# An attention and gate kernel on one core: the values of the first batch earlier in the order, and new weights of the order

## The chip, the cores and the metric

One core of a Trainium2 chip runs one program. Its engines are TensorE (PE, matmuls), VectorE (DVE), ScalarE (ACT), GpSimd (POOL) and SyncE (SP, which here issues all DMAs). Each engine works through its own list of instructions in order and waits on semaphores for the others. The metric is the device time of one execution in microseconds; the median of three runs before the change is 1022.07 us (1021.38 to 1022.09).

## The reference, cut to what matters

```python
kv_pool = kv.reshape(B, H//4, 4, W//4, 4, C).mean(axis=(2, 4))
kv_flat = kv_pool.reshape(B, -1, C) @ w_sr      # 768 keys, k = v
s = (q @ k.transpose(0, 2, 1)) / sqrt(C)
a = softmax(s)                                  # 1e-9 added to the sum
x = a @ v
gate = sigmoid(causal convolution of x with 5 taps per channel)
out = (gate * (x @ w_val)) @ w_out
```

There are 4 batches of 12288 queries and 128 channels, all in float32. Each batch has its own 768 keys, which are its values too.

## The kernel before, in words

The queries of a batch are cut into 24 groups of 512, and a group into 4 tiles of 128. For a tile PE makes the scores against 768 keys in six matmuls (L534): the high half of the query by the high and by the low half of the keys, and the low half of the query by the high half of the keys. The scores stay in one of three PSUM buffers (`s`). DVE takes their negative maximum (`nm`, L546), ACT the exponential and its sum (L553), DVE two small steps to the reciprocal (`r`, L562 and L567). ACT then writes the scaled high half in 16 bits (`hl`, L581), and DVE the low half (L592), after which the PSUM buffer is free. When two tiles are done, a DMA transpose (L605) on SP turns both halves into `pt`. When a group's two transposes have landed, 18 AV matmuls (L677) multiply by the high and the low half of the values (`vh`, `vl`). ACT copies the result to `x` (L695). GpSimd makes the five taps and adds them (`tap`, `gate`, L738 and L746; it also makes the low half of the query, `ql`, L520), ACT takes a tanh (`th`, L761), PE the value projection (`val`, L765), DVE their product (`h`, L769), PE the output projection (L774), and ACT the copy to `o` (L779), which SP stores. In the last groups DVE or PE make the taps and PE some of the transposes.

Per batch there is a `setup`. SP loads 16 pieces of `kv`; DVE (L307), and for some pieces of the first batch GpSimd (L326), sums each 4x4 window; PE projects (L360); ACT and DVE write the halves of the keys (`kh` L376, `kl` L400), and ACT the projected values as they are (`vt`, L388). The chain from there to the halves of the values is: `big`, the largest magnitude of each channel (DVE, L431); three steps on one column (L434, L436 and L438) that make a power of two `pw` and its inverse `up`; `diag`, the identity scaled by `up` (ACT, L423), and `wb`, the weights scaled by `pw` (ACT, L427); then for each half of the keys six matmuls of `vt` by `diag` (PE, L453), the high half `vh` (ACT, L463) and the low half `vl` (DVE, L474). The second half takes the same PSUM bank as the first.

The order of each engine's list is written by a planner (`Plan.order`) while the program is built. Every step has an engine, an estimated duration, a due time, the steps it comes after and the buffers it takes and frees. The planner goes forward in its own time. On each engine, among the steps that could begin within `WAIT` of the earliest one, it takes the one with the lowest due time. On SP a copy that follows a copy has `CLUMP` taken off its due time, so copies stay together. The due time of a step of a group is the group's number times `PERIOD`, plus its entry in `DUE` (four entries, one per tile, for the softmax steps, with a quarter of a period more for each). Loads and stores are placed on a grid of `PERIOD` and may not start before it. In `setup` the chain of the first batch has the due time `vals0` and an earliest start, `FIRST_VALS`:

```python
late = D["vals0"] if first else due(D["vals"])
s = plan.add("DVE", 0.87, late, lambda: v.tensor_reduce(
    out=big, in_=st["vt"], axis=AX.X, op=ALU.max, apply_absolute_value=True), vts,
    start=FIRST_VALS if first else 0.0)
...
by["wb"] = plan.add("ACT", 0.25, late + (20.0 if first else 1.0), wb, [s, weights_done], takes=("wb",))
```

Of the kernel before, what the change touches and what calls it, by code (L numbers as in the profile page):

```python
# [19 lines left out]
PIECES = 16  # L20
PARTS = 2

PERIOD = 9.97
DUE = dict(keys=-39.58, vals=-35.42, vals0=17.37, q=-44.21, qh=4.86, ql=-80.97,
           score=(-7.47, -6.32, -5.63, -6.47), max=(-23.77, -6.1, 13.1, -11.57),
           exp=(0.09, -30.82, -8.74, -13.77), hi=(-29.44, -20.58, 0.7, -43.56),
           lo=(22.34, -32.12, 5.51, 24.31), turn=(-11.32, 15.47, 2.1, 15.6), pe=6.0, thi=29.07,
           tlo=-11.13, r=(-50.81, -28.34, -47.73, -28.55), grid=-1.12, av=20.41, avs=4.86,
           halo=63.51, x=42.45, gate=30.41, th=53.25, val=47.33, h=-3.27, out=11.86, evac=21.59,
           store=52.32, end_diag=-56.57, end_gate=26.44, end_th=54.36, end_val=54.8, end_h=-26.7,  # L30
           end_out=56.32, end_evac=-38.92)

# [12 lines left out]
class Plan:  # L47
# [2 lines left out]

    EDGE = 0.04
    LAG = dict(PE=0.16, ACT=0.1, DVE=0.085, POOL=0.04, SP=0.0)
    WAIT = dict(PE=0.07, ACT=0.26, DVE=0.12, POOL=0.07, SP=0.8)
    DMA_LEAD, DMA_TAIL, CLUMP = 1.3, 0.8, 16.23

    def __init__(self):
        self.steps, self.stock = [], {}
# [14 lines left out]
    def order(self):  # L72
# [12 lines left out]
        while any(ready.values()):  # L85
            best = None
            for e, items in ready.items():
# [8 lines left out]
                if not ests:  # L96
                    continue
                t0 = min(t for t, _ in ests)
                s = min((s.due - (s.kind == last[e] == "copy") * self.CLUMP, n, s)
                        for n, (t, s) in enumerate(ests) if t <= t0 + self.WAIT[e])[2]  # L100
                t0 = next(t for t, x in ests if x is s)
# [52 lines left out]
def attn_moe_kernel(ctx, tc, qT, kvT, w_sr, w_moe, outT):  # L154
# [12 lines left out]
    HALO = TAPS - 1  # L167
    T = PERIOD
    D = DUE
    scale = 1.0 / float(C) ** 0.5  # L170
# [690 lines left out]

ON_PE, IN_S = 2, 4
TAIL, LAST, LAST_TURNED = 4, (2, 1, 1), ((), (0,), (0,))
FIRST_VALS, KEYS_BY = 26.0, -5
FIRST_Q = {0: 17.0, 1: 17.5, 2: 18.0, 4: 26.0}
SPARE, FOLDED = (6, 7, 8), (3, 5, 8, 10, 12)
TURNED = ((),)
# [28 lines left out]
```

## Time and profile before

| what | value |
|---|---|
| median of 3 runs | 1022.07 us |
| profiled execution | 1022.09 us, span 1020.2 us |
| busy, share of the span | PE 97%, DVE 91%, POOL 91%, ACT 87% |
| chain that ended last | PE 78%, POOL 5%, DVE 2%, ACT 1% |
| granted clock, mean | 0.995 |

The span is the time from the first to the last instruction; the rest of the profiled execution lies around it. A share of busy time is a mean over the whole span. The chain that ended last is followed back from the last instruction, at each step to what released it.

### The profile page before, as it was taken

How to read it: one execution, taken by the hardware profiler on the slowest of the kernel's cores; microseconds unless marked ns; L12 is line 12 of the kernel's file. 1: busy time of each engine (PE TensorE's matmuls, PEld its weight loads, DVE VectorE, ACT ScalarE, POOL GpSimd, SP SyncE). 2: the span in 40 equal slices, each digit the busy share in tenths (PEclk: the TensorE clock that was granted, in tenths of full speed). 3: DMA queues.
4: the chain of work that ended last, by engine and by line, in shares of the span. 5: the costliest groups of instructions: out<-in, count | busy, mean ns of one | idle time of the engine just before them, and what ended most of it. 6: DMA issues, size and time to landing. Idle time of an engine off the chain costs nothing.

```text
span 1020.2 us, 15459 instructions
## 1 busy us (share of the span) xinstructions
PE 991.6 (97%) x4586; PEld 606.9 (59%) x4586; DVE 930.5 (91%) x1806; ACT 884.9 (87%) x1584; POOL 930.6 (91%) x1069
## 2 busy tenths in 40 slices
PE   4799999999999999999999999999999999999998
PEld 3555555556555666656665656555666566666655
DVE  6899999999999999999999999999989898898984
ACT  1788889989898998999899989998999989999884
POOL 5179999999999999999999999999999999999994
PEclk9799999999999999999999999999999999999999
DMA  8699999999999999999999999999999999999983
GB/s 321 122 241 234 229 230 269 232 238 244 212 251 244 223 232 253 245 218 238 224 241 226 233 248 230 232 248 231 186 216 217 201 207 224 206 211 190 186 176 93
DMA packets 616994, 227.05 MB, mean 223 GB/s; under 512 B 595536, under 2 KB 596304, under 8 KB 616912
## 3 DMA queue, kind: packets, MB, share of 16 engines
q1 hardware_dynamic: 616912, 226.07, 103.2%
q8 instruction: 37, 0.61, 0.3%
q14 instruction: 45, 0.37, 0.1%
HBM read 50.66 MB, written 25.17 MB: 74 GB/s over the span
## 4 chain that ended last, share of the span: by engine, by line
PE 78%; POOL 5%; DVE 2%; ACT 1%; issue 0%; POOLq 0%; ACTq 0%; DVEq 0%
PE s L534 33%; PE av L677 30%; PE m L774 7%; PE m L765 7%; POOL gate L746 2%; POOL tap L738 1%; DVE hl L592 1%; POOL ql L520 1%; ACT hl L581 0%; DVE nm L546 0%; POOL gate L738 0%; PE m L453 0%; PE m L360 0%; ACT s L553 0%; PE s L824 0%
## 5 line engine op out<-in xcount | busy, mean ns | idle before, releaser
L746 POOL TENSOR_TENSOR gate<-gate,tap 128x512 f32<-128x512 f32 x376 | 481.7, 1281 | 10.0
L592 DVE SCALAR_TENSOR_TENSOR hl<-s,r,hl 128x768 f16<-128x768 f32 x382 | 386.2, 1012 | 30.9 <-ACT hl L581 29.8
L553 ACT ACTIVATE s<-s,nm 128x768 f32<-128x768 f32 x384 | 336.3, 876 | 49.7 <-DVE nm L546 49.1
L546 DVE TENSOR_REDUCE nm<-s 128x1 f32<-128x768 f32 x384 | 362.8, 946 | 17.3 <-PE s L534 16.2
L677 PE MATMUL av<-pt,vh 128*128 128x512 f16 (+2 forms) x1176 | 370.8, 377 | 0.5 <-ACT s L553 0.5
L581 ACT ACTIVATE hl<-s,r 128x768 f16<-128x768 f32 x382 | 339.6, 907 | 26.7 <-DVE r L567 15.8
L534 PE MATMUL s<-kh,qh 128*128 128x512 f32 (+1 forms) x768 | 261.0, 421 | 11.0 <-DVE hl L592 8.1
L738 POOL TENSOR_SCALAR tap<-x,wb 128x512 f32<-128x512 f32 x376 | 254.6, 698 | 0.0
L677 PE MATMUL av<-pt,vl 128*128 128x512 f16 (+2 forms) x588 | 220.1, 375 | 0.0
L534 PEld LDWEIGHTS s<-kh,qh 128*128 128x128 f32 x768 | 132.2, 191 | 130.2 <-issue 54.9
L534 PE MATMUL s<-kl,qh 128*128 128x512 f32 (+1 forms) x768 | 199.5, 341 | 0.0
L534 PE MATMUL s<-kh,ql 128*128 128x512 f32 (+1 forms) x768 | 198.3, 339 | 0.0
L677 PEld LDWEIGHTS <-vh 128*128 128x128 f16 x1176 | 107.5, 98 | 142.6 <-issue 55.4
L520 POOL TENSOR_TENSOR ql<-q,qh 128x512 fp32r<-128x512 f32 (+1 forms) x98 | 122.8, 1254 | 28.1 <-ACT qh L516 28.1
L534 PEld LDWEIGHTS s<-kh,ql 128*128 128x128 f32 x768 | 119.2, 190 | 17.4
L534 PEld LDWEIGHTS s<-kl,qh 128*128 128x128 f32 x768 | 119.1, 190 | 17.5 <-DVE kl L400 0.2
L774 PE MATMUL m<-h,wm 128*128 128x512 f32 x188 | 99.0, 608 | 0.2 <-DVE h L769 0.2
L677 PEld LDWEIGHTS <-vl 128*128 128x128 f16 x588 | 57.7, 98 | 68.3 <-issue 22.1
L765 PE MATMUL m<-x,wb 128*128 128x512 f32 x188 | 96.0, 592 | 0.0
L738 POOL TENSOR_SCALAR gate<-x,wb 128x512 f32<-128x512 f32 x94 | 65.5, 697 | 28.0 <-ACT x L695 27.7
L567 DVE RECIPROCAL r<-r 128x1 f32<-128x1 f32 x384 | 62.9, 164 | 13.1
L779 ACT ACTIVATE o<-m 128x512 f32<-128x512 f32 x94 | 56.2, 598 | 17.7 <-PE m L774 16.8
(67 smaller groups left out, 617.8 us busy)
## 6 DMA issues: line engine op xcount, KB each, us to landing
q<-in_q SPq DMA_DIRECT2D x47, 512.0 KB, 5.4
out<-o SPq DMA_DIRECT2D x47, 512.0 KB, 3.3
kvt<-in_kv SPq DMA_DIRECT2D x60, 384.0 KB, 4.2
pt<-hl SPq DMA_TRANSPOSE x191, 5.9
o<-in_kv SPq DMA_DIRECT2D x3, 384.0 KB, 8.3
q<-in_q SPq DMA_DIRECT2D x2, 256.0 KB, 5.8
kvt<-in_kv SPq DMA_DIRECT2D x2, 192.0 KB, 4.4
raw<-in_w_moe SPq DMA_DIRECT2D x1, 261.0 KB, 2.9
```

Of the source, the lines that this page charges most:

```text
L520: nc.gpsimd.tensor_tensor(out=g.ql, in0=g.io.q[:, mine], in1=g.qh.bitcast(F32), op=ALU.subtract)
L534: nc.tensor.matmul(t[:, c0:c1], a[:, sl], k[:, c0:c1], start=(i == 0), stop=(i == 2))
L546: v.tensor_reduce(out=s.tile, in_=sc.tile[:, :NK], axis=AX.X, op=ALU.max, negate=True)
L553: nc.scalar.activation(out=sc.tile[:, :NK], in_=sc.tile[:, :NK], func=AF.Exp, bias=mx.tile, accum_out=sc.tile[:, NK:NK + 1])
L567: v.reciprocal(out=s.tile, in_=e.tile)
L581: nc.scalar.activation(out=g.hls[j // 2][:, half, 0], in_=sc.tile[:, :NK], func=AF.Copy, scale=r.tile)
L592: v.scalar_tensor_tensor(out=hl[:, half, 1], in0=sc.tile[:, :NK], scalar=r.tile, in1=hl[:, half, 0], op0=ALU.mult, op1=ALU.subtract)
L677: nc.tensor.matmul(g.av, st[name][:, k * P:(k + 1) * P], g.pt[:, :, a * NCH + k], start=(i == 0), stop=(i == len(AV) - 1))
L738: nc.gpsimd.tensor_scalar(out=s.tile, in0=src(k), scalar1=wt(k), scalar2=1.0, op0=ALU.mult, op1=ALU.mult)
L746: nc.gpsimd.tensor_tensor(out=g.gate, in0=g.gate, in1=tap.tile, op=ALU.add)
L765: nc.tensor.matmul(g.m, st["wb"][:, :C], g.x[:, HALO:], start=True, stop=True)
L774: nc.tensor.matmul(g.m2, wout, g.h, start=True, stop=True)
```

## The change

Nothing that is computed changes, and no instruction is added or taken away. The due times, the period, two of the planner's constants and the earliest start of the first batch's chain from `vt` to `vh` and `vl` have other values. `vals0` goes from 17.37 to -59.66 and `FIRST_VALS` from 26 to 22.

```diff
-PERIOD = 9.97
-DUE = dict(keys=-39.58, vals=-35.42, vals0=17.37, q=-44.21, qh=4.86, ql=-80.97,
-           score=(-7.47, -6.32, -5.63, -6.47), max=(-23.77, -6.1, 13.1, -11.57),
-           exp=(0.09, -30.82, -8.74, -13.77), hi=(-29.44, -20.58, 0.7, -43.56),
-           lo=(22.34, -32.12, 5.51, 24.31), turn=(-11.32, 15.47, 2.1, 15.6), pe=6.0, thi=29.07,
-           tlo=-11.13, r=(-50.81, -28.34, -47.73, -28.55), grid=-1.12, av=20.41, avs=4.86,
-           halo=63.51, x=42.45, gate=30.41, th=53.25, val=47.33, h=-3.27, out=11.86, evac=21.59,
-           store=52.32, end_diag=-56.57, end_gate=26.44, end_th=54.36, end_val=54.8, end_h=-26.7,
-           end_out=56.32, end_evac=-38.92)
+PERIOD = 9.88
+DUE = dict(keys=-39.84, vals=-44.67, vals0=-59.66, q=-43.31, qh=-7.04, ql=-78.0,
+           score=(-7.1, -5.53, -6.34, -6.81), max=(-25.34, -9.07, 9.14, -15.56),
+           exp=(-3.41, -25.85, -12.4, -10.65), hi=(-37.79, -19.35, -1.17, -39.39),
+           lo=(21.28, -36.39, 7.1, 23.79), turn=(-9.59, 6.75, 10.86, 17.01), pe=3.81, thi=36.11,
+           tlo=-12.72, r=(-51.78, -33.05, -44.37, -42.65), grid=-0.11, av=19.88, avs=6.14,
+           halo=69.09, x=41.55, gate=30.73, th=60.74, val=47.67, h=-6.87, out=21.42, evac=28.89,
+           store=50.37, end_diag=-61.96, end_gate=34.22, end_th=46.53, end_val=51.12,
+           end_h=-30.5, end_out=51.42, end_evac=-42.17)
...
-    WAIT = dict(PE=0.07, ACT=0.26, DVE=0.12, POOL=0.07, SP=0.8)
-    DMA_LEAD, DMA_TAIL, CLUMP = 1.3, 0.8, 16.23
+    WAIT = dict(PE=0.06, ACT=0.29, DVE=0.12, POOL=0.05, SP=0.77)
+    DMA_LEAD, DMA_TAIL, CLUMP = 1.3, 0.8, 3.87
...
-FIRST_VALS, KEYS_BY = 26.0, -5
+FIRST_VALS, KEYS_BY = 22.0, -5
```

## Rows read from the trace of the kernel before

**Rows 1.** The page, busy time of PE, of its weight loads, and of DVE, ACT and POOL: us, share of the span, instructions.

```profile
PE 991.6 (97%) x4586; PEld 606.9 (59%) x4586; DVE 930.5 (91%) x1806; ACT 884.9 (87%) x1584; POOL 930.6 (91%) x1069
```

**Rows 2.** Busy time by stretch. Columns: stretch, its length, then for PE, PEld, DVE, ACT and POOL the busy us and, in brackets, the instructions; PE's granted clock (1.00 is 2.4 GHz), the DMA share, GB/s.

```profile
25.00:60.00 35.00, 26.83 (x113) 19.58 (x112) 29.80 (x58) 25.26 (x46) 7.50 (x8) 0.85 0.76 164
60.00:100.00 40.00, 38.03 (x177) 22.71 (x177) 37.33 (x76) 34.90 (x62) 37.58 (x43) 1.00 1.04 224
100.00:140.00 40.00, 39.13 (x178) 22.78 (x176) 38.54 (x76) 35.22 (x64) 38.62 (x44) 1.00 1.10 237
140.00:980.00 840.00, 839.43 (x3879) 509.61 (x3879) 784.58 (x1518) 760.79 (x1360) 808.63 (x916) 1.00 1.07 226
980.00:1020.00 40.00, 37.12 (x205) 22.91 (x204) 24.82 (x46) 23.96 (x47) 25.08 (x32) 1.00 0.52 128
```

**Rows 3.** What PE waited for: us in total, times, longest. The first line is of the stretch from 22 to 60 us, the others of that from 60 to 160 us.

```profile
PE s L534 <- DVE hl L592: 6.6, 4, 3.2
...
PE s L534 <- DVE hl L592: 1.5, 3, 0.9
PE s L534 <- DVE r L562: 1.1, 1, 1.1
```

**Rows 4.** What DVE waited for from 25 to 60 us, in the same columns.

```profile
DVE nm L546 <- PE s L534: 4.9, 5, 1.3
```

**Rows 5.** Single instructions on PE in order of time: start, us, engine, line, operation, out<-in, form, count, and in brackets the idle time ahead of it and what ended that.

```profile
31.67 0.98 PE L534 MATMUL s<-kh,qh 128*128 128x512 f32 x2 [3.24 <-DVE hl L592]
...
43.85 1.03 PE L453 MATMUL m<-diag,vt 128*128 128x128 f32 x6
...
48.17 0.61 PE L534 MATMUL s<-kh,qh 128*128 128x512 f32 x2 [1.19 <-DVE r L562]
...
49.83 0.62 PE L534 MATMUL s<-kh,qh 128*128 128x512 f32 x2 [0.35 <-DVE hl L592]
...
50.98 0.39 PE L677 MATMUL av<-pt,vh 128*128 128x512 f16 x1
...
52.17 0.59 PE L534 MATMUL s<-kh,qh 128*128 128x512 f32 x2 [0.15 <-DVE r L562]
...
771.38 0.38 PE L677 MATMUL av<-pt,vh 128*128 128x512 f16 x1
```

**Rows 6.** Busy time by stretch as in rows 2; the third column from the end is PE's granted clock.

```profile
22.00:28.00 6.00, 6.00 (x22) 4.87 (x23) 2.74 (x5) 3.26 (x7) 3.79 (x3) 1.00 0.27 102
28.00:34.00 6.00, 2.76 (x10) 2.17 (x9) 4.70 (x13) 4.27 (x7) 0.00 (x0) 0.72 0.32 96
...
46.00:52.00 6.00, 4.42 (x22) 2.87 (x22) 5.55 (x11) 5.34 (x11) 1.27 (x1) 1.00 0.90 204
```

**Rows 7.** Single instructions on DVE in order of time, columns as in rows 5.

```profile
25.54 0.96 DVE L546 TENSOR_REDUCE nm<-s 128x1 f32<-128x768 f32 x1 [1.32 <-PE s L534]
...
29.67 0.93 DVE L431 TENSOR_REDUCE big<-vt 128x1 f32<-128x768 f32 x1
30.52 1.93 DVE L592 SCALAR_TENSOR_TENSOR hl<-s,r,hl 128x768 f16<-128x768 f32 x2
...
33.97 0.96 DVE L546 TENSOR_REDUCE nm<-s 128x1 f32<-128x768 f32 x1 [1.20 <-PE s L534]
...
39.12 0.13 DVE L438 TENSOR_SCALAR up<-pw 128x1 int32<-128x1 int32 x1
...
50.55 0.55 DVE L474 TENSOR_TENSOR vl<-m,vh 128x384 f16<-128x384 f32 x1
```

**Rows 8.** Single instructions on ACT in order of time, columns as in rows 5.

```profile
29.26 1.70 ACT L581 ACTIVATE hl<-s,r 128x768 f16<-128x768 f32 x2
...
40.93 0.41 ACT L423 ACTIVATE diag<-ident,up 128x128 f32<-128x128 f32 x1
...
44.92 0.48 ACT L463 CAST vh<-m 128x384 f16<-128x384 f32 x1 [0.82 <-PE m L453]
...
57.60 0.60 ACT L695 ACTIVATE x<-av 128x512 f32<-128x512 f32 x1 [0.51 <-PE av L677]
```

**Rows 9.** Issues of DMA transposes on SP in order of time: start of the issue, us, engine, line. The first is the second of group 0, the other the second of group 71.

```profile
40.21 3.65 SPq L605 DMA_TRANSPOSE pt<-hl  x1
...
758.70 3.61 SPq L605 DMA_TRANSPOSE pt<-hl  x1
```

**Rows 10.** DMA issues by form: out<-in, engine, operation, count, median us from issue to landing.

```profile
pt<-hl SPq DMA_TRANSPOSE x191, 5.9
```

**Rows 11.** The chain that ended last, in order of time, in the fourth batch: start, us, engine, tile, line, matmuls.

```profile
961.07 0.43 PE av L677 x2
...
962.56 1.31 PE av L677 x6
...
964.98 2.17 PE av L677 x10
...
971.05 0.43 PE av L677 x2
```

**Rows 12.** The same chain in the tail.

```profile
1002.01 0.81 ACT pt L650
...
1003.79 0.94 DVE gate L720
...
1005.38 1.12 PE m L774 x2
```

## The prediction

> **What bounds the kernel now.** I read the busy shares first, then stretches of the span, then who waited for whom, and last the single instructions of the first 60 us. The page [rows 1] gives TensorE (PE) 991.6 us of 1020.2: the whole question is where the other 28.6 us are and whether PE's work itself can shrink. The stretches [rows 2] say where: PE is idle 8.17 us of the 35 us from 25 to 60, 1.97 us from 60 to 100, 0.87 us from 100 to 140, and 0.57 us in all of the 840 us from 140 to 980; the last 40 us hold 2.88 us. Before 25 us PE waits for the loads and sums of the first batch, which the edit doesn't touch. So from 140 to 980 us nothing is to be had from waits. What can be won lies between 25 and 140 us, 11.0 us of idle PE, and what can be lost lies anywhere.
>
> Between 25 and 140 us PE waits for VectorE (DVE): 6.6 us for `hl` (a score tile that comes free) before 60 us, and 1.5 and 1.1 us behind it from 60 to 160 [rows 3]. DVE in turn is busy 29.80 of 35, 37.33 of 40 and 38.54 of 40 us [rows 2], and of its own waits 4.9 us up to 60 us are for scores from PE [rows 4]. It is a ring of three score buffers: score on PE, maximum on DVE, exponential on ACT, reciprocal on DVE, high half on ACT, low half on DVE, next score. Whatever else stands in DVE's order there lengthens the ring.
>
> The clock makes it worse. PE did no work between its third score's end near 28.4 us and 31.67 [rows 5]; the granted clock was 1.00 (2.4 GHz) from 22 to 28, 0.72 from 28 to 34, a mixture of 2.4 and 1.2 GHz, and 1.00 again only from 46 us [rows 6].
>
> **The chain that is moved, and its price.** The first batch's chain is: `big` on DVE at 29.67 (0.93 us), three small steps of which the last, `up`, is at 39.12 (0.13 us), `diag` on ACT at 40.93, the first half's values on PE at 43.85 and their `vh` on ACT at 44.92, and the second half's `vl` on DVE at 50.55 (0.55 us) [rows 5, 7, 8]. Its arithmetic is under 5 us, yet it takes 21.4 us, from 29.67 to 51.10, since each small step stands behind a step of the softmax that could begin sooner. The first AV matmul begins at 50.98 [rows 5], within 0.12 us of the end of the second `vl`. What else it needs was there: the second transpose of group 0 is issued at 40.21, and from issue to landing the median is 5.9 us, so near 46.1 [rows 9, 10]. So the chain, and not the transposes, holds the first AV back by 4.9 us, and with it the first `x` at 57.60 [rows 8] and all of GpSimd's gate work.
>
> The edit takes the due time of the chain from 17.37 to -59.66 and its earliest start from 26 to 22. In DVE's order `big` can then stand behind the last `kl`, whose end is near 24.2, in the 1.32 us in which DVE waits for the first score, until 25.54 [rows 7]. I add up what that does:
>
> 1. `big` leaves the place in front of the first `hl`, which starts at 30.52. The high half that this needs is the first of two in 1.70 us from 29.26 [rows 8], so it ends near 30.1 and `hl` can come at 30.15: 0.4 us earlier, and the fourth score with it. Upper bound 0.85 us, `big`'s whole slot from 29.67 to 30.52. Against it, a `vl` of 0.55 us may come in front of a softmax step there: lower bound -0.6 us. DVE has waits of its own to take them (1.20 us before 33.97 [rows 7]), so I take **0.4 us**.
> 2. The values matmuls move into PE's idle 3.24 us before 31.67 [rows 5]. The first half's row has 1.03 us, partly at 1.2 GHz, so both are 2.1 us, and the idle time covers it. With the cover gone it would cost all of that. I count **0**.
> 3. The first AV has no chain to wait for. PE is idle 1.19, 0.35 and 0.15 us ahead of the scores at 48.17, 49.83 and 52.17 [rows 5], 1.69 us together, while a group's 18 AV matmuls, 3.9 us by the steady rows (10 in 2.17 us, [rows 11]), lie ready. Bounds 0 and 1.69; I take **1.5 us**, since a matmul of 0.22 us fills such a gap with little left over.
> 4. Behind that, `vl` (1.0 us of DVE) and the values have left the stretch in which DVE has no room, and `x`, the gates and so `val` and `out` come up to 5 us sooner as filling. PE's idle time from 60 to 140 is 2.84 us [rows 2]. What remains for PE to wait for is `hl`, which earlier filling only shifts; I take half, **1.4 us**, with bounds of 0 and 2.84.
>
> The sum is 3.3 us. `wb` moves with the chain; ACT is busy 25.26 of the 35 us [rows 2] and has room for it at either place.
>
> **The other weights.** All due times change, so the order could change anywhere. For the steady stretch it can be worked out. PE's order repeats with the period, so I take each due time modulo it. Old (9.97): scores at 1.00, 2.50, 6.14 and 9.32, AV from 0.47 in 18 steps of 0.27, `val` at 7.45. That gives 2 AV, score, 6 AV, score, 10 AV, score, `val`, score, `out`, and these are the rows at 961 to 971 us, 9.98 us a round [rows 11]. New (9.88): scores at 0.60, 2.78, 6.82 and 8.48, AV from 0.12 in steps of 0.34, `val` at 8.15. Again 2, 6 and 10 AV between the same scores, `val` between the third and the fourth. `out` is overdue as soon as it is ready in both. With the same sequence PE's time is the same: **0 us** for the steady part. It can't gain more than the 0.57 us of waits and a little of what switching between kinds of matmul costs; what it could lose is bounded by the slack of the transposes: the second one of group 71 is issued at 758.70, plus 5.9, and its AV begins at 771.38, so 6.8 us late in the span [rows 5, 9]. CLUMP (copies kept together) falls from 16.23 to 3.87, so loads and transposes alternate more on SP; at the end of the span the grid of loads, at 9.88 us a group against 9.98 of real time, has run ahead by 96 x 0.10 = 9.6 us, which the free buffers cap. A transpose behind a load that waits would eat that slack first: taken as 0, with an upper bound of 9.6 - 6.8 = 2.8 us. In the tail PE is idle 2.88 us [rows 2] and every `end_` weight is new: 0, bounds -1 and +2.
>
> The profiled execution took 1022.09 us, 1.9 us over its span, and the median of the runs is 1022.07: the same. 1022.1 - 3.3 = **1018.8 us**.
>
> **A rule of the skill.** The granted clock fell from 1.00 to half in the stretch that holds the idle time before 31.67 [rows 5, 6]. The Trainium skill (TensorE: Matmul & The Clock Gate, Part 1) says that an idle array is throttled to half rate and activity releases it. By that rule the values matmuls in the gap would keep the clock up, which gives the sum another 2 us (the first rival). No run here shows yet whether they come early enough.
>
> **Rivals.**
> - *The clock stays up.* For it: the values matmuls fall into the very gap after which it fell. Against: `diag` has to be there before 30 us. Of DVE's 4.9 us of waits for scores [rows 4], 1.32 us are for the first; 1.20 us of the rest stand before 33.97, behind the score of 31.67 [rows 7]. A bit over half of the other 3.6 us would go: 1018.8 - 2.0 = 1016.8 us.
> - *The chain stays strung out.* Each small DVE step is ready a little after the one before it, and a ready maximum goes ahead; before the edit 8.6 us lie from the end of `big`, at 30.52, to `up` at 39.12 [rows 7]. If `big` misses the idle DVE before 25.54, the chain gains about 5 us of its 21 and only item 3 in part: 1021.2 us.
> - *It is given back at the end.* From 1002.01 to 1005.38 the chain at the end runs ACT, DVE, DVE, PE over one group's transposed scores, gate and output [rows 12], 3.4 us, in which PE has the AV of another group to do. If the new `end_` weights put that AV elsewhere, up to 3.2 us return: 1022.0 us.
> - *Slower: waits at the head of DVE's order.* From `diag` (40.93) to `vh` (44.92) the first half takes 4.0 us, with ACT idle 0.82 us for PE in it [rows 8]. If `vl` stands in DVE's order ahead of a maximum or an `hl` that is ready, DVE waits for PE and ACT, and the ring stops. For two halves that is 2 x 2.5 us of pure chain (an estimate from the rows: `diag` 0.41, values 1.03, `vh` 0.48, `vl` 0.55) against the 1.20 us that DVE idles there anyway: 3.8 us more, and DVE has none to spare up to 140 us. 1025.9 us. It decides when the fourth score begins after 31.67. The Trainium skill (TensorE: Matmul & The Clock Gate, section Architectural detail, on queue depths) has ACT and DVE strictly first in, first out, which is what makes such a wait possible.
>
> **Chances.** The forecast, 2 to 5 us won: 0.48, with its own range 1016.9 to 1020.0. The clock stays up: 0.12. Strung out 0.12, given back 0.11, slower 0.17 (with the loads before transposes in it). About 0.2%, 2.0 us, is what can be told from no change, so faster means below 1020.0 and slower above 1024.1: faster 0.60, same 0.25 (with 0.02 from the slow case at its small end), slower 0.15. The range reaches over the clock case on one side and over the given-back case and the small end of the slow one on the other: 1015.6 to 1023.0.
>
> **What would show it.** Right: `big` starts before 25.6 us, the second `vl` ends before 42, the first AV starts by 47, PE's idle time from 25 to 140 falls from 11.0 to about 8 us, the order of 2, 6 and 10 AV stands in batch 3 with 9.98 us a round, and the last group's times move by the same 3 us. Wrong: the fourth score starts later than 31.67; `up` is still behind 35 us; PE waits for transposes; PE's idle time after 980 us exceeds 2.88.

## The result, and the profile after

The changed kernel takes 1030.97 us (median of 4 runs, 1029.61 to 1031.74), the kernel before 1021.91 (4 runs, 1021.38 to 1022.09): a ratio of 1.0094, 95% interval 1.0081 to 1.0107. It is slower by 9 us where 3 us faster was forecast. The profiled execution took 1030.81 us, with a span of 1028.9 us.

The page after, PE's busy line beside [rows 1] and the shares of the chain that ended last:

```profile
PE 993.4 (97%) x4586; PEld 607.1 (59%) x4586; DVE 930.2 (90%) x1806; ACT 884.8 (86%) x1584; POOL 928.9 (90%) x1069
...
PE 81%; DMA 7%; DVE 5%; POOL 3%; ACT 1%; issue 1%; SPq 1%; ACTq 0%; DVEq 0%; POOLq 0%
```

The instructions are the same and nearly as long; PE is idle 1028.9 - 993.4 = 35.5 us where it was 28.6. The other 1.8 us of the longer span are PE's busy time; they are not tied to its order, since in e13, e14 and e17 below PE has the same order and is busy 990.9 to 991.3 us. A share of 7% for DMA stands in the chain, 4% of it transposes (`pt`). The chain before could be followed back only to 138 us and has no DMA from there on. Where the idle time lies is read from stretches. First after, with the columns of [rows 2] and the long stretch cut at 720 us:

```profile
25.00:60.00 35.00, 26.07 (x114) 18.79 (x113) 29.00 (x59) 25.72 (x47) 6.55 (x7) 0.90 0.74 155
60.00:100.00 40.00, 38.43 (x177) 22.47 (x176) 38.38 (x76) 35.81 (x63) 38.42 (x45) 1.00 1.11 228
100.00:140.00 40.00, 40.00 (x187) 24.23 (x186) 39.01 (x77) 36.40 (x66) 38.62 (x44) 1.00 1.09 232
140.00:720.00 580.00, 571.68 (x2629) 344.16 (x2627) 541.79 (x1053) 514.72 (x919) 548.58 (x622) 1.00 1.12 233
720.00:980.00 260.00, 259.82 (x1202) 159.37 (x1201) 233.02 (x450) 236.16 (x426) 250.50 (x286) 1.00 1.03 206
980.00:1029.00 49.00, 45.89 (x247) 28.44 (x245) 32.48 (x60) 31.32 (x60) 32.55 (x41) 1.00 0.60 131
```

And before, the two stretches that [rows 2] holds as one:

```profile
140.00:720.00 580.00, 579.56 (x2675) 350.25 (x2676) 551.75 (x1071) 524.35 (x935) 558.74 (x632) 1.00 1.10 236
720.00:980.00 260.00, 259.87 (x1206) 159.36 (x1204) 232.83 (x447) 236.44 (x426) 249.89 (x285) 1.00 1.02 203
```

Length less busy time is PE's idle time. From 25 to 60 us it is 8.93 (before 8.17), from 60 to 140 us 1.57 (2.84), from 720 to 980 us 0.18 (0.13). The last rows stop 0.2 us before the end of the span before and 0.1 us behind it after; from 980 us to the end of the span it is 3.0 (3.1). From 140 to 720 us, the rest of the first three batches, it is 8.32, and it was 0.44. So the loss is there, in the stretch in which PE had next to no idle time before; all other stretches together are idle 1.0 us less than before. What PE waited for from 140 to 720 us after, the four longest (before there was one wait of 0.9 us, which ends at 140.33 us):

```profile
PE av L677 <- DMA pt<-hl: 4.5, 5, 2.4
PE av L677 <- ACT s L553: 1.7, 2, 1.3
PE s L534 <- DVE r L562: 0.8, 2, 0.5
PE m L774 <- DVE h L769: 0.8, 1, 0.8
```

The first line is a wait that the kernel before does not have at all: AV matmuls that wait for a transpose. The second line hides another of them: the 1.3 us end at 184.14 us, and by the records of the DMA the transpose of these AV matmuls landed at 184.01. The longest, on PE, on SP and on DVE (group 9, counted from 0):

```profile
143.30 0.38 PE L677 MATMUL av<-pt,vh 128*128 128x512 f16 x1 [2.42 <-DMA pt<-hl]
```

```profile
134.24 0.53 SPq L505 DMA_DIRECT2D q<-in_q  x1
134.85 0.38 SPq L802 DMA_DIRECT2D out<-o  x1
135.33 13.53 SPq L605 DMA_TRANSPOSE pt<-hl  x3
```

```profile
145.55 0.96 DVE L546 TENSOR_REDUCE nm<-s 128x1 f32<-128x768 f32 x1 [2.75 <-PE s L534]
```

The group's second transpose goes out at 135.33 behind a load and a store, and its AV matmul begins only at 143.30. The AV stands at the head of PE's list, so the scores behind it don't run, and DVE idles 2.75 us for the next score. PE, which idled 0.44 us of this stretch before, has nowhere to make that up. The same transpose and the same AV matmul before:

```profile
133.31 9.78 SPq L605 DMA_TRANSPOSE pt<-hl  x2
```

```profile
143.36 0.39 PE L677 MATMUL av<-pt,vh 128*128 128x512 f16 x1
```

There the transpose stood behind copies too, and by the records it landed at 141.85, 1.5 us before its AV. After, it lands at 143.17, 1.3 us later, and PE comes to its AV at 140.88, 2.5 us sooner.

SP is a list without much slack as well: by the records its issues fill 536 of these 580 us before and 559 after, transposes alone 483 and 507. And the DMA share is 1.10 before and 1.12 after, so the times of the packets add up to more than the 16 engines' whole time. No run made SP's list or the DMAs' work shorter for the whole stretch (in e17, with the stores on ACT, SP's issues still fill 554 us), so whether one of these two sets the pace beside PE and DVE is not shown.

### The profile page after: what moved, and what is told of

Read it like the earlier page. It is cut to its first block, busy times and chain, and to the rows that moved or that the text cites. A ratio compares the mean times of both kernels' runs of the same rounds, so it can differ in the third digit from the quotient of the medians.

```text
span 1028.9 us, 15468 instructions
## 1 busy us (share of the span) xinstructions
PE 993.4 (97%) x4586; PEld 607.1 (59%) x4586; DVE 930.2 (90%) x1806; ACT 884.8 (86%) x1584; POOL 928.9 (90%) x1069
## 4 chain that ended last, share of the span: by engine, by line
PE 81%; DMA 7%; DVE 5%; POOL 3%; ACT 1%; issue 1%; SPq 1%; ACTq 0%; DVEq 0%; POOLq 0%
PE s L534 34%; PE av L677 31%; PE m L774 7%; PE m L765 7%; DMA pt<-hl 4%; DVE hl L592 2%; DMA kvt<-in_kv 2%; DVE nm L546 2%; POOL gate L746 1%; DMA o<-in_kv 1%; ACT hl L581 1%; POOL tap L738 1%; DVE h L769 1%; DVE pool L307 0%; SPq L289 0%
```

## The experiments

All ratios are to the kernel before, run on the same chip, with their 95% interval. "Idle" is PE's idle time from 140 to 720 us of the profiled execution, 580 less its busy time in that row. The runs of one kernel differ by 1 to 5 us (e6 by 11), and the profiled one is not always the middle one: in e4, e8 and e14 it is the slowest, 2.4 to 3.1 us over the median. So small differences in it are not to be read. Each expectation says itself what its theories hold.

| run | median us | ratio (95% interval) | idle, us |
|---|---|---|---|
| after | 1030.97 | 1.0094 (1.0081 to 1.0107) | 8.3 |
| e1 | 1028.28 | 1.0066 (1.0045 to 1.0087) | 5.7 |
| e2 | 1025.75 | 1.0042 (1.0025 to 1.0058) | 2.2 |
| e3 | 1026.44 | 1.0042 (1.0027 to 1.0057) | 4.9 |
| e4 | 1029.74 | 1.0080 (1.0058 to 1.0102) | 7.6 |
| e5 | 1128.00 | 1.1047 (1.1031 to 1.1063) | 55.2 |
| e6 | 1129.90 | 1.1071 (1.1038 to 1.1104) | 49.4 |
| e7 | 1023.29 | 1.0014 (1.0006 to 1.0023) | 0.3 |
| e8 | 1026.10 | 1.0048 (1.0032 to 1.0064) | 4.8 |
| e9 | 1039.06 | 1.0175 (1.0158 to 1.0192) | 15.9 |
| e10 | 1021.43 | 1.0003 (0.9991 to 1.0015) | 0.1 |
| e11 | 1026.12 | 1.0040 (1.0025 to 1.0055) | 1.7 |
| e12 | 1031.58 | 1.0099 (1.0084 to 1.0114) | 8.0 |
| e13 | 1030.25 | 1.0084 (1.0065 to 1.0103) | 10.6 |
| e14 | 1026.84 | 1.0045 (1.0029 to 1.0061) | 8.5 |
| e15 | 1025.56 | 1.0040 (1.0024 to 1.0055) | 2.7 |
| e16 | 1028.26 | 1.0059 (1.0044 to 1.0074) | 6.6 |
| e17 | 1035.14 | 1.0137 (1.0121 to 1.0152) | 13.2 |
| e18 | 1023.28 | 1.0021 (1.0010 to 1.0032) | 2.2 |

**The two parts apart (e1, e2).** e1 is the kernel before with the early chain alone, e2 the kernel after with the old start of the chain.

```diff
# e1, in the kernel before
-vals0=17.37
+vals0=-59.66
-FIRST_VALS, KEYS_BY = 26.0, -5
+FIRST_VALS, KEYS_BY = 22.0, -5
# e2, in the kernel after: the same two lines the other way
```

> The kernel before with the chain alone: vals0 -59.66, FIRST_VALS 22, all else old. Theory L (the loss comes from the other weights, which put AV matmuls closer behind the landing of their transposes; the chain by itself is harmless): 1019 to 1022 us, PE's idle time from 140 to 720 us under 1.5 us. Rival C (the early chain shifts the whole order and is the cause): 1027 to 1031 us, with PE stalls for transposes between 140 and 200 us. If the forecast's items 1, 3 and 4 hold for the chain: 1018.8 us.

> The kernel after with the old chain: vals0 17.37, FIRST_VALS 26, all other weights new. Theory L: still slow, 1027 to 1032 us, with the same small stalls of PE for transposes in the second and third batch. Rival C: back to 1022 us.

Both are slower than before, by 0.7% and 0.4%, so neither part alone carries the loss. But changing two numbers of the first batch's chain (e1) brought 5.7 us of idle time between 140 and 720 us, long after the chain. The planner had written the whole order anew.

**The chain alone, the rest kept (e7).** Here the kernel before keeps its order step by step, and only the chain and the first ten AV matmuls of group 0 are moved early, near to where the change has them but not to the same places: here the first `vl` goes behind the first two `hl`, and the second half's values behind the sixth score instead of the third (line numbers move by one to three).

```diff
+    behind(big, st["kls"][1], *st["vts"])
...
+    behind(d0, pe[2], diag)
+    behind(vh0, g0.his[1], d0)
+    behind(vl0, g0.los[0], g0.los[1], vh0)
+    behind(d1, pe[5], vl0)
...
+    for n, s in enumerate(g0.avs[:10]):
```

> The order of the kernel before with only the first batch's chain moved by hand: big and its three steps behind the last kl, diag behind them, the first values behind the third score, the first vl behind the first two hl, the second values behind the sixth score, and ten of the first group's AV matmuls in front of the scores at 48 to 52 us. Everything after 60 us keeps its order. The forecast's items 1, 3 and 4: 1018 to 1020 us. Rival R (the ring is bound by DVE and PE's gain is taken back by 140 us): 1021 to 1022.5 us. Rival C of the first four runs (an early chain by itself costs time): 1026 us or more.

The stretch from 25 to 60 us of e7, and what its scores waited for from 22 to 60 us:

```profile
25.00:60.00 35.00, 25.46 (x115) 17.99 (x114) 29.28 (x59) 26.30 (x49) 8.47 (x9) 0.95 0.76 162
```

```profile
PE s L534 <- DVE hl L593: 7.8, 7, 3.4
```

The ratio is 1.0014: no gain, rather a loss of 0.6 to 2.3 us by the interval. The time lies between what rival R and rival C expected. From 140 to 720 us PE is idle 0.25 us, as before; from 25 to 60 us it is idle 9.54 us where it was 8.17, although the granted clock is 0.95 there instead of 0.85. It waits for `hl` 7.8 us instead of 6.6 [rows 3]: the fourth score begins at 31.21 us, 0.46 us sooner than before, but one that follows, at 40.43, waits 3.37 us. The early chain, placed so, wins nothing in the stretch it was made for. What e1 lost beyond that lies in its new order, with 5.7 us of idle time from 140 to 720 us where e7 has 0.3.

**Single constants of the planner (e3, e4, e8, e12, e10, e11).** Each is one line: e3 and e8 put the new `CLUMP` and the new `WAIT` into the kernel before, e4 and e12 the old ones into the kernel after; e10 and e11 change the period of the kernel before by 0.01.

```diff
# e3, before                # e4, after
-CLUMP 16.23                -CLUMP 3.87
+CLUMP 3.87                 +CLUMP 16.23
# e8, before: WAIT = dict(PE=0.06, ACT=0.29, DVE=0.12, POOL=0.05, SP=0.77)
# e12, after: WAIT = dict(PE=0.07, ACT=0.26, DVE=0.12, POOL=0.07, SP=0.8)
# e10, before               # e11, before
-PERIOD = 9.97              -PERIOD = 9.97
+PERIOD = 9.96              +PERIOD = 9.98
```

> The kernel before with CLUMP 3.87 alone. Theory L (slack between landing and AV is lost through the due times of AV and scores): 1022 to 1024 us. Rival K (loads and transposes alternate more on SP, and a transpose behind copies lands 2 to 2.5 us later): 1026 to 1031 us with PE waits for transposes of 3 us or more.

> The kernel after with CLUMP 16.23 alone put back. Theory L: 1027 to 1031 us. Rival K: 1020 to 1023 us, and PE's waits for transposes gone.

> The kernel before with the new WAIT alone (0.01 to 0.03 us of the planner's reckoning; no due time changes). Theory S (the old weights are one lucky order: any new order has some AV matmuls right behind their transposes and loses 3 us or more): 1025 to 1029 us with late transposes. Rival (only weights that move AV or the chain matter): 1021 to 1023 us.

> The kernel after with the old WAIT alone put back (0.01 to 0.03 us). Theory S: another order of the same kind, anywhere from 1025 to 1032 us, PE's idle time from 140 to 720 us 2 to 9 us. If the new WAIT were the cause: back to 1022 us.

> The kernel before with PERIOD 9.96 for 9.97, nothing else. Theory S (the old weights are one order that happens to have next to no step standing ahead of work that is ready; nearly every other order has a few, whatever was changed): 1024 to 1028 us, PE's idle time from 140 to 720 us 2 us or more against 0.44. Rival P (only the large moves of the change cost time): 1021 to 1023 us.

> The kernel before with PERIOD 9.98 for 9.97. Theory S: 1024 to 1028 us. Rival P: 1021 to 1023 us.

Neither `CLUMP` nor `WAIT` carries the loss: put back to its old value in the kernel after, each leaves it at 8 to 10 us. In the kernel before each costs 4 to 5 us, and so does a period longer by 0.01. Only e10 keeps its time, and it is no test of theory S: its order is that of before on DVE, ACT and GpSimd, and only 4 of 4586 places on PE and 3 of 358 on SP differ. e4 tells the most. What PE waited for transposes in it from 140 to 720 us:

```profile
PE av L677 <- DMA pt<-hl: 0.7, 2, 0.5
```

That was 4.5 us in the kernel after. But PE waits 3.3 us for `r` and 2.2 for `hl` instead, is idle 7.6 us, and the time is still 8 us above before. So the waits for transposes can go without the loss going. What is waited for differs: from 140 to 720 us PE waits 3.3 us for `h` in its output projections in e3, 3.1 us for `h` and 2.0 for a transpose in e8, and for transposes above all in the kernel after. The weights of before give an order with next to no waits in the first three batches. The four others that were made from it by one or two numbers and did change the order (e1, e3, e8, e11) lose 4 to 7 us each. In e11 only 1.3 of the 4 us are idle time from 140 to 720 us; the rest lies in other stretches and in PE's busy time (993.3 us).

**The AV matmuls behind the next score (e9).** In the kernel after, in 11 late groups, the AV matmuls ahead of the next score go behind it, so that a late transpose no longer stops a score.

```diff
+    for i in (9, 11, 13, 26, 32, 34, 38, 48, 56, 58, 62):
+        first = order.index(groups[i].avs[0])
+        after = next(s for s in order[first:] if s in scores)
+        ahead = [s for s in groups[i].avs if order.index(s) < order.index(after)]
...
+        order[at:at] = ahead
```

> The order of the kernel after; in the 11 groups of the first three batches whose AV began within 0.4 us of the landing of their second transpose, the AV matmuls that stand ahead of the next score go behind it. Nothing else is moved. Theory H (PE stands at the head of its list at an AV whose transpose is late, while a score that is ready stands behind it, and DVE then waits for that score): PE's waits for transposes fall from 4.5 to about 1 us, its idle time from 140 to 720 us from 8.3 to about 3 us, 1024 to 1026.5 us. Rival (the score behind it would have had to wait as well, since DVE and the score buffers set the pace): 1029 to 1031 us.

What PE waited for from 140 to 720 us in e9, where AV has the line 678:

```profile
PE s L534 <- DVE hl L592: 11.0, 9, 1.4
PE av L678 <- DMA pt<-hl: 1.8, 2, 1.5
```

The wait for transposes fell from 4.5 to 1.8 us, and 11.0 us of waits for `hl` came in its place, nine of up to 1.4 us: a score that comes before those AV matmuls comes before its buffer is free. The AV matmuls were what PE had to do in that time. The slack on one side is the other side's filling; that idea for a repair fell.

**Copies and transposes on SP (e5, e6, e13 to e16).** First the copies directly ahead of each second transpose were put directly behind it, 46 in the kernel after (e5) and 44 in that of before (e6).

```diff
+    for turn in turns[1::2]:
+        i = sp.index(turn)
+        while i and sp[i - 1].kind == "copy" and sp.index(turn) > 30:
...
+            order.insert(b, order.pop(a))
```

> The order of the kernel after, with one thing moved: where copies stand on SP directly ahead of a group's second transpose, they go directly behind it (46 places). Nothing else is planned anew. Theory T (PE's stalls of the second and third batch come from second transposes that land late behind copies, 8 to 10 us after their issue instead of 5.6): PE's waits for transposes go from 4.5 us to under 1 us, its idle time from 140 to 720 us from 8.2 to under 3 us, 1022 to 1025 us. Rival O (the order on the engines is itself worse, the late transposes only show it): 1028 to 1031 us.

> The same move in the kernel before (44 places). Theory T: nothing waits for transposes there, so 1021 to 1023 us; if the move frees slack that nothing used, the same time. Rival: copies behind the second transpose delay the next group's first one and the loads, 1023 to 1026 us.

Both lost over 10%. What DVE waited for most in e5, over the whole span:

```profile
DVE pool L307 <- DMA kvt<-in_kv: 78.8, 24, 5.1
```

The loads of `kv` that start one transpose later stand at the head of DVE's list as window sums that cannot begin, and behind them the softmax. The Trainium skill (TensorE: Matmul & The Clock Gate, section Architectural detail, on queue depths) calls DVE strictly first in, first out; these 78.8 us agree. As a test of the transposes the two runs tell nothing, since the loads' lateness covers all else.

Then the other way: copies that stand between a group's two transposes start ahead of the first, where what they wait for allows it. e13: the 11 late groups of the kernel after; e14: the 4th to the 71st group of it; e15 the same in the kernel before; e16 the same in e1.

```diff
+    for i in range(3, 71):
+        first, second = turns[2 * i], turns[2 * i + 1]
+        run = sp[sp.index(first) + 1:sp.index(second)]
+        for copy in run:
+            at = order.index(first)
+            if all(order.index(n) < at for n in copy.needs):
+                order.remove(copy)
+                order.insert(at, copy)
```

> The kernel after, its list unchanged except for 11 groups of the first three batches whose AV products wait for their second transpose or nearly (9, 11, 13, 26, 32, 34, 38, 48, 56, 58, 62): there the loads and stores that SP starts between the group's first and second transpose are started ahead of the first instead, where what they wait for allows it. Nothing else moves. Theory T (the transposes behind copies are the cause): these second transposes land near 5.6 us after their issue, the waits of AV products for them fall from 4.5 us to under 2, the idle time of PE from 140 to 720 us falls from 8.3 to 4 to 6, and the time is 1026 to 1029 us. Theory U (PE and DVE both follow fixed lists without slack, and the late transpose is only the place where it shows): the waits go elsewhere, to scores that wait for halves, and the time stays at 1029 to 1032 us.

> The same move in all groups from the 4th to the 71st of the kernel after. Theory T: no AV product waits for a transpose that stood behind a copy; PE's idle time from 140 to 720 us falls from 8.3 to about 3 and the time to 1022 to 1026 us. Theory U: 1028 to 1033 us, with the waits of AV products for transposes gone and others in their place. Loads that start earlier may also push first transposes back by 2 to 2.5 us, which have more slack; if those become the late ones, 1033 to 1040 us.

> The same move in the kernel before, in all groups from the 4th to the 71st. Before has next to no idle time from 140 to 720 us (0.44), so there is nothing to win: both theories expect 1021 to 1023 us if the move itself is harmless. If it reads 1026 or more, the move itself costs, and e14 has to be read against that.

> The same move in the kernel of e1 (the kernel before with the early chain alone, 1028.3 us, 5.7 us of idle time from 140 to 720 us). Theory T: 1022 to 1025 us. Theory U: 1027 to 1030 us.

Theory T fell in this form: e13 keeps the time of the kernel after and e16 that of e1. The waits for transposes from 140 to 720 us in e14:

```profile
PE av L677 <- DMA pt<-hl: 7.3, 5, 2.5
```

They are longer than in the kernel after, though its median is 4.1 us shorter (the profiled execution, the slowest of five, only 1.6): the copies now push back the first transpose, and that the second, since they follow each other on SP. The group that waits near 142 us has its first transpose on SP from 128.72 to 135.60 us there, behind two loads of `kv` and one of the query, and its second from 136.31 on. The control e15 is not harmless either: 4 us lost in the kernel before, more than expected. Near 142 and 182 us AV matmuls wait in the kernel after, in e13 and in e14 alike.

**The stores off SP (e17, e18).** The stores of line 802 are issued by ACT on its own queue, at their old place in the order, in the kernel after (e17) and before (e18).

```diff
-            plan.add("SP", 1.6, at, start=at, run=lambda: nc.sync.dma_start(
+            plan.add("SP", 1.6, at, start=at, run=lambda: nc.scalar.dma_start(
```

> The kernel after, its order unchanged, except that the stores of line 802 (one for two groups, all but those of the last groups) are issued by ACT, on its own DMA queue, at the place in the order that they had on SP; ACT made their data itself, so it waits for nothing there. This takes them out of SP's list. Theory V (SP is nearly full in the first three batches and its transposes come late behind copies): SP's transposes have fewer copies ahead, PE's idle time from 140 to 720 us falls from 8.3 to 2 to 5, and the time is 1024 to 1028 us. Theory U (PE and DVE follow fixed lists without slack; the late transposes are only where it shows): 1029 to 1032 us, and more if the issue on ACT costs what it does on SP (0.4 to 0.5 us each, some 45 of them, ahead of exponentials): 1033 or above.

> The same in the kernel before, whose PE idles 0.44 us from 140 to 720 us. Theory V: nothing to win there, 1021 to 1022 us, if the issue on ACT is free; this is the control for e17. If ACT's issues cost, 1024 us or above, and e17 has to be read against that. Theory U expects the same two cases.

For e17, PE's waits for transposes from 140 to 720 us, and the times from issue to landing of all transposes:

```profile
PE av L677 <- DMA pt<-hl: 8.6, 6, 2.4
```

```profile
DMA to landing us min/median/max: 5.4/6.4/14.1
```

For e18 the only wait of PE in that stretch, and the same times:

```profile
PE av L677 <- ACT s L553: 2.1, 1, 2.1
```

```profile
DMA to landing us min/median/max: 4.5/6.3/13.2
```

Theory V fell: off SP's list the stores run beside the transposes, which take longer (median 6.4 instead of 6.0 us, longest 14.1 instead of 10.0). But the pair tells more than either theory asked, because the same disturbance meets both orders. The one wait of e18 is for a transpose too: the 2.1 us end at 144.13 us, and by the records the transpose landed at 143.99, issued at 130.79 with a store of ACT's beside it (the exponential that the row names is another part of the same wait). So in the order of before one transpose came too late, by 2.1 us, and the median grew by 2.0 us. In the order of after the waits for transposes grew by 4.1 us and the median by 4.2 us. So in both the medians grew by about what the AV matmuls waited longer, which fits an old order with room for all but the worst of the late transposes. It is two pairs of numbers: in e17 the idle time grew by 4.9 us, with 2.1 us more for `r` in it.

## Why the prediction was wrong

**The step that failed: "0 us for the steady part", with 2.8 us as its upper bound.** It had two legs. The first was that the due times, taken modulo the period, give the same sequence of 2, 6 and 10 AV matmuls between the scores. In the fourth batch that is so; the chain that ended last, in order of time:

```profile
959.74 0.43 PE av L677 x2
...
961.22 1.31 PE av L677 x6
...
963.65 2.17 PE av L677 x10
...
969.71 0.43 PE av L677 x2
```

A round is 9.97 us there, as before, and PE idles 0.18 us from 720 to 980. It was put to the whole steady part. Until 676 us, the last start of a load of `kv` after, window sums, projections of the next keys and loads stand among the same steps, and the sum left them out. From 140 to 720 us PE is idle 8.32 us instead of 0.44, and that is where the runs put the loss.

The second leg was the slack of the transposes, 6.8 us, from group 71 [rows 5, 9]. That is the last group of the third batch, after the loads. For each group I took the start of the first AV matmul less the landing of its second transpose, from the records: the median is 7.2 us in the fourth batch in both kernels, but before it is 3.0, 4.2 and 4.4 in the first three, and after 2.6, 3.2 and 3.3. Less than 0.3 us have 1 group before and 9 after. The bound of 9.6 - 6.8 should have been made with the smallest slack in the trace, 0.3 us (group 58), not with one late group. And transposes are not the whole of it: the sum had no term for scores that wait for `r` and `hl`, which take their place in e4 and e9.

**Items 1 to 4: 3.3 us forecast, 0.5 us seen.** PE's idle time from 25 to 140 us fell from 11.0 to 10.5 (from the start to 140 us by 1.0, since the first score began 0.4 us sooner). The steps themselves came as worked out, on DVE and on PE after:

```profile
23.71 0.94 DVE L431 TENSOR_REDUCE big<-vt 128x1 f32<-128x768 f32 x1
...
30.23 0.54 DVE L474 TENSOR_TENSOR vl<-m,vh 128x384 f16<-128x384 f32 x1
31.09 1.94 DVE L592 SCALAR_TENSOR_TENSOR hl<-s,r,hl 128x768 f16<-128x768 f32 x2 [0.32 <-ACT hl L581]
32.95 0.55 DVE L474 TENSOR_TENSOR vl<-m,vh 128x384 f16<-128x384 f32 x1
```

```profile
28.64 0.83 PE L453 MATMUL m<-diag,vt 128*128 128x128 f32 x6
30.82 0.94 PE L453 MATMUL m<-diag,vt 128*128 128x128 f32 x6 [1.35 <-DVE vl L474]
32.16 0.62 PE L534 MATMUL s<-kh,qh 128*128 128x512 f32 x2 [0.40 <-DVE hl L592]
...
36.52 0.61 PE L534 MATMUL s<-kh,qh 128*128 128x512 f32 x2 [1.97 <-DVE hl L592]
...
39.90 0.98 PE L534 MATMUL s<-kh,qh 128*128 128x512 f32 x2 [2.06 <-DVE hl L592]
...
45.98 0.39 PE L677 MATMUL av<-pt,vh 128*128 128x512 f16 x1
...
55.61 0.58 PE L534 MATMUL s<-kh,qh 128*128 128x512 f32 x2 [1.76 <-DVE r L562]
```

- Item 1, 0.4 us won: 0.6 lost. `big` left its place (23.71), but a `vl` came ahead of the first `hl`, which starts at 31.09 instead of 30.52, and the fourth score at 32.16 instead of 31.67 [rows 5, 7]. That is the lower bound, and the slower rival's mechanism at a price of 0.5 us where 3.8 was named. e7, with that `vl` behind the `hl`, has the 0.4 us.
- Item 2, 0: right. The first half's values lie in the gap, the second half's wait 1.35 us there for the first `vl`, whose bank they take, and the score behind them still waits for `hl`.
- Item 3, 1.5 us: the first AV begins at 45.98 instead of 50.98 (by the records the second transpose landed at 47.65 before, not near 46.1, so the chain held the AV back by 3.3 us and not by 4.9), and of 1.69 us of idle time ahead of three scores 0.36 is left (ahead of the score at 48.46). But the scores at 36.52, 39.90 and 55.61 wait 1.97, 2.06 and 1.76 us, and from 25 to 60 us PE idles 0.8 us more than before. So filling moved a wait to a later place in the ring of three buffers. e7 shows the same with the rest of the order kept.
- Item 4, 1.4 us: 1.27 seen from 60 to 140 us, so the number came out. But in e7 that stretch is idle 3.06 us (before 2.84), so it isn't shown to come from the chain, and it may be luck.

The chain's own work, called under 5 us, is 5.8 us by the rows if both halves are counted, as the second waits for the first's bank; nothing in the sum hangs on it.

**The rivals.** The clock, after, in the columns of [rows 6]:

```profile
28.00:34.00 6.00, 4.24 (x26) 3.54 (x25) 4.74 (x12) 5.15 (x10) 0.09 (x1) 1.00 0.19 74
34.00:40.00 6.00, 1.96 (x11) 1.27 (x9) 5.05 (x10) 5.15 (x9) 1.19 (x1) 0.90 0.69 131
40.00:46.00 6.00, 5.85 (x19) 4.54 (x20) 3.97 (x8) 2.73 (x6) 0.00 (x0) 0.53 0.91 174
```

The granted clock stayed at 1.00 from 28 to 34 us, where it had been 0.72, and fell to 0.53, close to the 1.2 GHz level, from 40 to 46 us, after the waits of 1.97 and 2.06 us. The 2 us of that rival did not follow: in e7 the clock is 0.95 from 25 to 60 us and the time no shorter, because the scores wait for DVE. The trace agrees in both stretches with what the Trainium skill (TensorE: Matmul & The Clock Gate, Part 1) says, that an idle array is throttled and activity releases it: matmuls in the gap and 1.00, then the gaps and 0.53. Strung out it was not (`up` at 25.98 instead of 39.12), and given back at the end neither: from 980 us to the end of the span PE is idle 3.0 us, before 3.1. Of the four signs named for "wrong", two came: the fourth score is late, and PE waits for transposes. (The 2.88 of the fourth stops 0.2 us short of the span's end, so 3.11 against it says nothing.) Only the second has to do with the loss, and not as its sole cause.

What stays open is which of the new due times takes the slack from the transposes; no run changed `DUE` beyond `vals0`. That the whole of the 8.3 us would go with earlier transposes is not shown either: every run that moved steps on SP or PE made other waits, and in e4, almost without waits for transposes, the loss stayed. No version tried beats the kernel before.

## What to carry to other kernels

Where two engines run in-order lists without idle time and a third part (here a DMA transpose) joins them, read the slack of that join for every group, by stage, and bound a new order with the smallest, not with a median or a late group; then look for what waits in its place once that slack is mended. A change of a planner's weights is a new order everywhere: keep the old order and move the one chain by hand, as e7 did, to price the chain itself. Where PE idles in a ring of buffers, work put into its gap won nothing here, since the engine that frees the buffers had no less ahead of it.

## What the runs showed of the hardware

- A DMA transpose takes SP 3.7 us in the median before (2.8 to 7.7) and 4.0 after, and more behind copies: by the records from 140 to 720 us the mean before is 3.7 us directly behind another transpose, 4.3 us behind one copy, 5.4 behind three and 6.3 behind four or more. All transposes together hold SP 778 us before and 823 us after (sums of their records).
- Stores on ACT's queue still ran into the transposes on SP's: the longest time to landing rose from 10.0 to 14.1 us (e17) and from 9.7 to 13.2 (e18). An issue took ACT 0.34 us in the median, and SP 0.57 us.
- Starting copies, loads of `kv` among them, one transpose later cost over 100 us (e5, e6).
